# Three longer lags in the order planner of a fused attention and mixture-of-experts kernel

## The chip, the cores and the metric

The kernel runs on one core of a Trainium2 chip. The metric is the device time of one execution in microseconds (us); lower is better. The engines are TensorE (PE), ScalarE (ACT), VectorE (DVE), GpSimd (POOL) and SyncE (SP), and each works off a queue of its own in order.

## The reference

Three layers follow each other on 1152 tokens (2 batches of 576) of width 512:

```
scores = q @ k.T / 8                      # 2 batches, 8 heads, 576 x 576
keep the 32 largest of each row, softmax over them, x = attn @ v
x = prelu(x @ w_in, alpha) @ w_out        # 512 -> 2048 -> 512
logits = x @ w_gate + log1p(exp(x @ w_noise)) * noise
the top 2 of 8 experts for each token, weights = softmax over the two
out[token] = sum over its two experts e: weight * (relu(x @ w1[e]) @ w2[e])   # 512 -> 1024 -> 512
```

## The kernel before

**An order planned in Python.** The kernel writes no schedule by hand. Each piece of work is a Python generator that yields steps: `(engine, cost, lag, ...)`, a lock to take, or a mark to wait for. The class `Order` (L135 on) plays these generators through a simulated clock while the kernel is being built. An engine that is free in the simulation takes the waiting step with the lowest rank. The step's instructions are emitted at that moment, so the order of the simulation becomes the order of each engine's queue on the chip. In `dispatch` the generator's next step becomes known only after the step's cost, a small hop, and the lag:

```
wait = HOP if nxt[0] != eng else STEP if eng in (DVE, ACT, POOL) else 0.0
self.at(end + wait + (req[2] if len(req) > 2 else 0.0), 0, lambda: self.handle(p, nxt))
```

A lag is therefore a guess at how long a transfer takes after its issue. It does not become an instruction. The waits that the chip performs come from the data dependencies, whatever the plan assumed. Costs and lags are constants near the top of the file, in us.

**The expert stage.** Attention and the first layer fill roughly the first 580 us. Then the eight experts follow each other, each with up to 336 tokens in slots. TensorE works in the same pattern for each expert `e` in eight blocks: the hidden part (`expert_block`, L1506, into the banks `h_ps` and `s_ps` in turn), then the output part (L1541, `y` and `x_ps`; L1548 for expert 7). Values are split in two float32r halves, so ACT makes `hh` from a hidden bank (L1517), DVE the rest `hl` (L1522), and both feed the output part. ACT and DVE also split the experts' weights (`w2i`, `w2o`, L1297 and L1300). The steps for `hh` and `hl` carry a rank lowered by 50 and go first where the planner has a choice.

Three round trips through DRAM run beside this:

- *Input rows* (`gather_x`). GpSimd gathers an expert's rows from `x2` into `xg` (L1322). For experts 2 to 7 SP then moves them, quarter by quarter, into the buffers `xh0`, `xl0` (lock `x0`, L1339). After the lag XW, DVE transposes them (L1349), and ACT and DVE split them into the expert's input `xeh` and `xel` (L1364, L1366).
- *Partner rows* (`gather_partner`). Each token has two experts. When expert `e - 1` is in `ysc`, GpSimd gathers for expert `e` those rows that the tokens' other expert produced earlier (L1579). After a lag of DG + GX, ACT scales them with the partner's weight (L1587).
- *Own rows* (`expert_out`). For experts 1 to 6 the output stands transposed. DVE turns it in blocks (L1608), SP writes it to `ysc` (L1615) and reads it back in row order into `wo0`, `wo1` (L1625). After a lag, DVE multiplies with the own weight and adds the partner part (L1636), and GpSimd scatters the sum to the output (L1667).

The gathers of L1322 use the lag GX as well; it stays as it is.

Of the kernel before, what the change touches and what calls it, by code (L numbers as in the profile page):

```python
# [62 lines left out]
MB, MP = 0.0, 0.0  # L63
FILL = 0.8
FS = 3.0
XC, XR, NX, GX, XW = 0.65, 30.0, 2, 5.0, 2.5
XN, LC = 60.0, 35.0
YT = (1, 7)
GB3, NRW = 2, 5
DG, DX, DS = 1.0, 2.0, 0.5  # L70
YC, YL = 0.65, 4.0
NK, FB1 = 4, 12.0
BEGIN = (("DMA", 1.7), ("ACT", 1.9), ("DVE", 1.5), ("POOL", 1.0))


# [33 lines left out]
PE, ACT, DVE, POOL, DMA = "PE", "ACT", "DVE", "POOL", "DMA"  # L109
# [5 lines left out]
def act(n, bias=0):  # L115
    return 0.1 + n * 0.00083 + 0.09 * bias
# [6 lines left out]
def dve(n):  # L123
    return 0.07 + n / 960
# [6 lines left out]
def rows(j):  # L131
    return min(CP, CAP - j * CP)


class Order:  # L135
# [99 lines left out]
    def take(self, *names, room=1):  # L235
        def got():
            for w in names:
                if self.held.get(w, 0) < room:
                    self.held[w] = self.held.get(w, 0) + 1
                    return w  # L240
        return "until", got

    def give(self, what):
        self.held[what] -= 1
        self.given[what] = self.now
        self.at(self.now, 1, self.scan)

    def mark(self, *what):
        self.made.add(what)
        self.at(self.now, 1, self.scan)  # L250

    def need(self, *what):
        return "until", lambda: what in self.made
# [9 lines left out]
def block_kernel(ctx: ExitStack, tc: tile.TileContext, q, k, v, w_in, w_out, alpha,  # L263
# [19 lines left out]
    order = Order()  # L283
    for eng, t in BEGIN:
        order.free[eng] = t
# [1277 lines left out]
    def pieces(*tags):  # L1563

        ts = [split(a2.tile([128, 2, 512], R32, name=t)) for t in tags]
        return [ts[0][:, 0], ts[0][:, 1], ts[1][:, 0]]

    def gather_partner(e):

        yield need("b1")  # L1570
        yield need("ysc", e - 1)
        tags = ("wi0", "wi1") if e % 2 else ("wi2", "wi3")
        for t in tags:
            yield take(t)
        PG[e] = pieces(*tags)
        mv = room["mv"]
        for j in range(CJ):
            yield POOL, 1.04
            nc.gpsimd.indirect_dma_start(  # L1579
                out=PG[e][j][0:rows(j)], out_offset=None, in_=ysc[0:e * WIDTH + 1],  # L1580
                in_offset=bass.IndirectOffsetOnAxis(ap=mv[0:rows(j), e, j, 2:3], axis=0),
                bounds_check=e * WIDTH, oob_is_err=False)
        yield DMA, DG, GX
        for j in range(CJ):
            yield ACT, act(512)
            r = rows(j)
            nc.scalar.activation(PG[e][j][0:r], PG[e][j][0:r], AF.Copy, scale=mv[0:r, e, j, 4:5].bitcast(F32))  # L1587
        yield FIN
        mark("pg", e)

    def to_ysc(e, own):

        yv = ysc[1 + e * WIDTH:1 + (e + 1) * WIDTH]
        nc.sync.dma_start(yv[0:2 * CP].rearrange("(j p) d -> p j d", p=CP), own[:, 0:2])
        nc.sync.dma_start(yv[2 * CP:CAP], own[0:CAP - 2 * CP, 2])

    def expert_out(e):
        turned = YT[0] <= e < YT[1]
        if e < E - 1 or turned:
            yield need("y2d", e, 7)  # L1600
        if turned or not e:
            yield take("yo", room=2)
            yo = room["b1"].tile([128, CJ, DM], F32, name="yo", bufs=2)
        if turned:
            t = yo.rearrange("p j d -> p (j d)")[:, 0:4 * WIDTH].rearrange("p (n b i) -> p n b i", b=4, i=32)
            for b in range(4):
                yield DVE, dve(WIDTH)
                V.transpose(t[:, :, b, :], YP[e][b][:, 0:WIDTH].rearrange("p (n s) -> p n s", s=32))  # L1608
            yield FIN
            give("y")  # L1610
            give("x_ps")
            yv = ysc[1 + e * WIDTH:1 + (e + 1) * WIDTH].rearrange("(n s) d -> s n d", s=32)
            for q in range(4):
                yield "issue", YC
                nc.sync.dma_start(yv[:, :, 128 * q:128 * q + 128], t[32 * q:32 * q + 32].rearrange("p n b i -> p n (b i)"))  # L1615
            yield DMA, DX, YL
            yield FIN
            mark("ysc", e)
            for w in ("wo0", "wo1"):
                yield take(w)  # L1620
            own = pieces("wo0", "wo1")
            yv = ysc[1 + e * WIDTH:1 + (e + 1) * WIDTH]
            yield DMA, 1.5, 2.0
            for j in range(CJ):
                nc.sync.dma_start(own[j][0:rows(j)], yv[j * CP:j * CP + rows(j)])  # L1625
            give("yo")
        if e:
            yield need("pg", e)
        for j in range(CJ):
            r = rows(j)  # L1630
            if e == E - 1 and not turned:
                yield need("y7", j)
            if e:
                yield DVE, dve(512)
                own_j = own[j][0:r] if turned else YP[e][j][0:r]
                V.scalar_tensor_tensor(PG[e][j][0:r], own_j, room["mv"][0:r, e, j, 1:2].bitcast(F32), PG[e][j][0:r],  # L1636
                                       op0=OP.mult, op1=OP.add)
                order.add(ranks["out", e], scatter_out(e, j, PG[e][j]))
            else:
                if j < NE:  # L1640
                    yield need("st", e)
                yield ACT, act(512)
                nc.scalar.activation(yo[0:r, j, :], ST[e] if j < NE else YP[e][j][0:r], AF.Copy)
        yield FIN
        if not turned:
            give("y")
        else:
            give("wo0")
            give("wo1")
        if not turned and e + 1 < E:  # L1650
            yield DMA, 2.1, YL
            to_ysc(e, yo)
            yield "lag0", 0.1
            yield FIN
            mark("ysc", e)
        if not e:
            give("yo")
        if e:
            for j in range(CJ):
                yield need("out", e, j)  # L1660
            for t in ("wi0", "wi1") if e % 2 else ("wi2", "wi3"):
                give(t)

    def scatter_out(e, j, res):
        mv = room["mv"]
        yield POOL, 1.04
        st = nc.gpsimd.indirect_dma_start(  # L1667
            out=out, out_offset=bass.IndirectOffsetOnAxis(ap=mv[0:rows(j), e, j, 3:4], axis=0),
            in_=res[0:rows(j)], in_offset=None, bounds_check=N - 1, oob_is_err=False)
        for o in out_sc:  # L1670
            tc.declare_no_dep(st.ins, o.ins, reason="every row is written once")
        out_sc.append(st)
        yield DMA, DS, 2.0
        yield FIN
        mark("out", e, j)
# [145 lines left out]
    for e in range(E):  # L1821
        te = t + e * TE
        if e < NX:
            ranks["xe", e] = te - 12.0
            order.add(te - 12.0, x_parts(e))
        if e >= NH:
            order.add(te - (XR if e >= NX else XN), gather_x(e))
        for ch in range(4):
            for half in range(2):
                order.add(te + (2 * ch - 4 + half) * FB, weights2(e, ch, half))  # L1830
        for fb in range(8):
            order.add(te + fb * FB, expert_block(e, fb))
        if e:
            order.add(te + 4 * FB, gather_partner(e))
        ranks["out", e] = te + TE
        order.add(te + TE, expert_out(e))
# [221 lines left out]
```

## Time and profile before

| what | value |
|---|---|
| median of 3 runs | 821.95 us (821.02 to 824.26) |
| profiled execution | 821.84 us, of which the span is 820.1 us |
| TensorE busy | 756.5 us, 92% |
| VectorE busy | 607.2 us, 74% |
| ScalarE busy | 506.8 us, 62% |
| GpSimd busy | 356.9 us, 44% |
| mean granted clock of TensorE | 0.965 |

The span reaches from the first to the last instruction of the profiled execution. The engines overlap, so their busy times don't add up to it. A row of a timeline is one instruction, or a few alike; what stands in brackets is the time for which its engine stood idle before it and what it waited for. The table of waits gives for each pair the total in us, how often, and the longest.

### The profile page before, as it was taken

What the parts mean: (1) busy time and instruction counts of PE and PEld (TensorE: products, weight loads), DVE (VectorE), ACT (ScalarE), POOL (GpSimd) and SP (SyncE); (2) the same over time, 40 slices, a digit from 0 to 9 for tenths busy, and PEclk for the clock granted to TensorE, in tenths of its full rate; (3) what the DMA queues carried; (4) which work ended last, traced back from release to release, by engine and by line L of the source; (5) the groups of instructions that cost most, each with busy time, mean ns of one, the idle gap of its engine ahead of it and who ended that gap; (6) DMA issues with size and microseconds to landing.
All of it is one profiled execution on the core that took longest, in us unless ns stands there. A gap on an engine that the chain in (4) does not pass through costs nothing. (4 is left out here: it accounts for less than half of the span.)

```text
span 820.1 us, 15508 instructions
## 1 busy us (share of the span) xinstructions
PE 756.5 (92%) x5238; PEld 690.0 (84%) x5238; DVE 607.2 (74%) x1713; ACT 506.8 (62%) x1081; POOL 356.9 (44%) x402
## 2 busy tenths in 40 slices
PE   8999878779999999999999999989797999999994
PEld 6888867668898998899988988778797999999983
DVE  6999989998988888988899353366547667767541
ACT  6878897887598778576657443454435455545430
POOL 3654665665575554464445334304231243312331
PEclk9999898778999999999999999999998999999998
DMA  9444689851445403573366388969896888986640
GB/s 272 137 154 121 193 290 306 282 181 66 129 164 183 144 26 104 168 240 132 107 191 219 128 242 315 326 179 234 211 244 174 237 258 233 277 234 187 190 125 32
DMA packets 99851, 156.62 MB, mean 191 GB/s; under 512 B 15902, under 2 KB 65582, under 8 KB 99764
## 3 DMA queue, kind: packets, MB, share of 16 engines
q1 hardware_dynamic: 94260, 145.04, 57.6%
q0 software_dynamic: 5504, 10.51, 4.4%
q8 instruction: 43, 0.70, 0.4%
q14 instruction: 44, 0.36, 0.1%
HBM read 126.76 MB, written 29.34 MB: 190 GB/s over the span
## 5 line engine op out<-in xcount | busy, mean ns | idle before, releaser
L671 POOL TENSOR_TENSOR low<-s_sb,low 128x576 f32<-128x576 f32 x72 | 102.4, 1423 | 82.1 <-ACT low L669 80.5
L947 PE MATMUL h_ps<-xh,wi 128*128 128x256 f32 (+1 forms) x576 | 124.0, 295 | 3.0 <-DVE gf L965 2.2
L947 PEld LDWEIGHTS h_ps<-xh,wi 128*128 128x128 f32 x576 | 97.9, 196 | 8.5 <-DVE gf L965 4.3
L632 DVE MAX8 tk<-rest 128x8 f32<-128x296 f32 x216 | 97.8, 459 | 1.1
L991 PE MATMUL y<-wo,gh 128*128 128x512 f32 x288 | 95.9, 414 | 0.2
L978 POOL TENSOR_TENSOR gl<-gf,gh 128x256 fp32r<-128x256 f32 (+1 forms) x80 | 56.5, 709 | 67.3 <-ACT gh L975 65.0
L716 PE MATMUL x_ps<-vb,pT 128*128 128x64 f32 (+1 forms) x640 | 81.0, 273 | 4.1 <-ACT pT L695 3.7
L716 PEld LDWEIGHTS x_ps<-vb,pT 128*128 128x128 f32 (+1 forms) x640 | 76.0, 190 | 10.3 <-ACT pT L695 7.0
L947 PE MATMUL h_ps<-xl,wi 128*128 128x256 f32 (+1 forms) x288 | 83.4, 290 | 0.0
L1297 ACT ACTIVATE w2o<-raw 128x512 fp32r<-128x512 f32 (+1 forms) x60 | 40.4, 710 | 62.2 <-PE x_ps L1541 46.4
L1300 DVE TENSOR_TENSOR w2o<-raw,w2o 128x512 fp32r<-128x512 f32 (+1 forms) x60 | 45.6, 792 | 39.2 <-ACT w2o L1297 38.9
L1541 PE MATMUL y<-hh,w2o 128*128 128x336 f32 (+1 forms) x288 | 68.1, 321 | 6.8 <-ACT hh L1517 6.8
L635 DVE MATCH_REPLACE8 rest<-tk,rest 128x296 f32<-128x296 f32 x144 | 64.9, 451 | 0.0
L1506 PE MATMUL h_ps<-xeh,w2i 128*128 128x336 f32 (+1 forms) x256 | 64.7, 314 | 0.0
L675 ACT ACTIVATE low<-low,bias 128x576 f32<-128x576 f32 x72 | 55.7, 773 | 12.1 <-POOL low L671 12.1
L581 PE MATMUL s_ps<-kp,qt 128*128 128x288 f32 (+2 forms) x336 | 61.2, 311 | 1.7 <-DVE rest L615 1.7
L1506 PE MATMUL s_ps<-xeh,w2i 128*128 128x336 f32 (+1 forms) x256 | 62.1, 310 | 0.0
L597 ACT ACTIVATE s_sb<-s_ps 128x576 f32<-128x576 f32 x72 | 46.8, 650 | 23.5 <-PE s_ps L581 22.9
L1579 POOL DMA_INDIRECT wi<-ysc,meta x21 | 25.1, 1195 | 82.7 <-DMA ysc<-yo 62.9
L669 ACT ACTIVATE low<-s_sb,bias 128x576 f32<-128x576 f32 x72 | 55.6, 774 | 8.8 <-POOL bias L640 8.7
L991 PE MATMUL y<-wo,gl 128*128 128x512 f32 x144 | 58.0, 403 | 2.0 <-POOL gl L978 1.9
L947 PEld LDWEIGHTS h_ps<-xl,wi 128*128 128x128 f32 x288 | 56.6, 197 | 0.7 <-issue 0.3
(315 smaller groups left out, 2077.0 us busy)
## 6 DMA issues: line engine op xcount, KB each, us to landing
raw<-in_moe_w_dram SPq DMA_DIRECT2D x60, 512.0 KB, 4.5
wi<-wsc SPq DMA_DIRECT2D x48, 512.0 KB, 4.3
wo<-wsc SPq DMA_DIRECT2D x48, 512.0 KB, 4.2
raw<-in_moe_w_in_dram SPq DMA_DIRECT2D x16, 512.0 KB, 4.4
raw<-in_moe_w_out_dram SPq DMA_DIRECT2D x16, 512.0 KB, 4.2
wsc<-wi SPq DMA_DIRECT2D x16, 512.0 KB, 4.2
wsc<-wo SPq DMA_DIRECT2D x16, 512.0 KB, 3.9
raw<-in_moe_w_dram SPq DMA_DIRECT2D x48, 128.0 KB, 5.4
```

The lines of the kernel that those rows point to most:

```text
L581: nc.tensor.matmul(s_ps[:, j, o:o + c1 - c0], l, r[:, c0:c1], start=(i == 0), stop=(i == len(steps) - 1 and (c < 4 or c1 != S)))
L632: V.max(tk[:, 8 * i:8 * i + 8], src)
L635: V.match_replace(rest, tk[:, 8 * i:8 * i + 8], src, -3.0e38)
L669: nc.scalar.activation(low, SC[ht], AF.Relu, bias=bi[:, 1:2], scale=-BIG)
L671: nc.gpsimd.tensor_sub(low, SC[ht], low)
L675: nc.scalar.activation(low, low, AF.Exp, bias=bi[:, 0:1], scale=SCALE, accum_out=SM[part][:, col:col + 1])
L716: nc.tensor.matmul(o, pT[:, i, cs], vb[b, hh // 2][:, s, i * 64:(i + 1) * 64], start=(first and hh == h and i == 0), stop=False)
L947: nc.tensor.matmul(h_ps, l[:, d, :], r[:, d, 0:gn], start=(n == 0), stop=(n == 11))
L978: nc.gpsimd.tensor_sub(gl, gf, split(gh))
L991: nc.tensor.matmul(Y1[g][t], l[:, t * 128:(t + 1) * 128], r, start=(i == 0 and n == 0), stop=(i == 15 and n == 2))
L1506: nc.tensor.matmul(h_ps, l[:, d, s * 128:(s + 1) * 128], r[:, d, :], start=(n == 0), stop=(n == 11))
L1541: nc.tensor.matmul(YP[e][b][:, 0:c], l[:, s, bs], r[:, 0:c], start=(fb == 0 and n == 0), stop=(fb == 7 and n == 2))
```

## The change

Three lags of the plan become longer. XW, the lag after the moves of gathered rows, goes from 2.5 to 4.0. The lag after the partner gathers was GX, 5.0, and is now a constant of its own, PL, of 10.0. The lag after the own rows are read back was 2.0, and is now OL, 8.0. No instruction is added, taken away or altered; the order in the engines' queues may differ from the first affected step on.

```diff
-XC, XR, NX, GX, XW = 0.65, 30.0, 2, 5.0, 2.5
+XC, XR, NX, GX, XW = 0.65, 30.0, 2, 5.0, 4.0
...
+OL, PL = 8.0, 10.0
...
                 in_offset=bass.IndirectOffsetOnAxis(ap=mv[0:rows(j), e, j, 2:3], axis=0),
                 bounds_check=e * WIDTH, oob_is_err=False)
-        yield DMA, DG, GX
+        yield DMA, DG, PL
         for j in range(CJ):
             yield ACT, act(512)
...
             yv = ysc[1 + e * WIDTH:1 + (e + 1) * WIDTH]
-            yield DMA, 1.5, 2.0
+            yield DMA, 1.5, OL
             for j in range(CJ):
                 nc.sync.dma_start(own[j][0:rows(j)], yv[j * CP:j * CP + rows(j)])
```

## Rows read from the trace of the kernel before

**Rows 1.** The page: its first line.

```profile
span 820.1 us, 15508 instructions
```

**Rows 2.** Stretches: busy us by engine, then granted clock, DMA share, GB/s.

```profile
650.00:680.00 30.00, 27.44 (x176) 26.61 (x175) 22.18 (x39) 14.04 (x27) 15.40 (x13) 1.00 0.90 278
680.00:710.00 30.00, 30.00 (x198) 30.00 (x197) 22.26 (x38) 15.48 (x29) 11.49 (x10) 1.00 0.89 251
```

**Rows 3.** The table of waits from 585 us to the end.

```profile
ACT wi L1587 <- DMA wi<-ysc,meta: 10.0, 3, 6.9
...
PE y L1541 <- ACT hh L1517: 6.8, 2, 6.1
...
DVE wi L1636 <- DMA wo<-ysc: 5.8, 3, 3.3
...
PE y L1541 <- DVE hl L1522: 2.9, 3, 1.5
...
DVE xl L1349 <- DMA raw<-in_moe_w_dram: 0.9, 1, 0.9
```

**Rows 4.** TensorE's timeline: start us, us, instruction [idle before it <- releaser].

```profile
619.67 0.65 PE L1541 MATMUL y<-hh,w2o 128*128 128x336 f32 x1 [6.05 <-ACT hh L1517]
...
624.95 0.40 PE L1506 MATMUL h_ps<-xeh,w2i 128*128 128x336 f32 x1
...
653.19 0.42 PE L1541 MATMUL y<-hl,w2o 128*128 128x336 f32 x1 [1.46 <-DVE hl L1522]
...
668.71 0.57 PE L1541 MATMUL y<-hh,w2o 128*128 128x336 f32 x2 [0.78 <-ACT hh L1517]
...
739.71 0.42 PE L1541 MATMUL y<-hl,w2o 128*128 128x336 f32 x1 [1.13 <-DVE hl L1522]
```

**Rows 5.** ACT's timeline around the first stall.

```profile
615.27 0.72 ACT L1587 ACTIVATE wi<-wi,meta 128x512 f32<-128x512 f32 x1 [6.93 <-DMA wi<-ysc,meta]
616.60 0.72 ACT L1587 ACTIVATE wi<-wi,meta 128x512 f32<-128x512 f32 x1 [0.61 <-DMA wi<-ysc,meta]
...
619.52 0.43 ACT L1517 ACTIVATE hh<-s_ps 128x336 fp32r<-128x336 f32 x1
...
621.10 0.30 ACT L1364 ACTIVATE xeh<-xl 128x128 fp32r<-128x128 f32 x1
```

**Rows 6.** DVE's timeline around the second and the last stall.

```profile
650.77 0.75 DVE L1636 SCALAR_TENSOR_TENSOR wi<-wo,meta,wi 80x512 f32<-80x512 f32 x1 [0.22 <-DMA wo<-ysc]
...
738.49 0.75 DVE L1636 SCALAR_TENSOR_TENSOR wi<-wo,meta,wi 128x512 f32<-128x512 f32 x1 [3.33 <-DMA wo<-ysc]
```

**Rows 7.** ACT's timeline around the third stall.

```profile
666.05 0.72 ACT L1587 ACTIVATE wi<-wi,meta 80x512 f32<-80x512 f32 x1 [2.50 <-DMA wi<-ysc,meta]
```

**Rows 8.** The tile wo: its loads' times from issue to landing.

```profile
DMA to landing us min/median/max: 2.9/4.9/6.8
```

**Rows 9.** GpSimd's timeline around the first stall.

```profile
603.65 1.40 POOL L1322 DMA_INDIRECT xg<-x,meta  x1 [16.93 <-DMA raw<-in_moe_w_dram]
...
607.95 1.02 POOL L1579 DMA_INDIRECT wi<-ysc,meta  x1 [0.31 <-issue]
...
610.82 0.97 POOL L1579 DMA_INDIRECT wi<-ysc,meta  x1 [0.30 <-issue]
```

**Rows 10.** Line 1579: its gathers' times from issue to landing.

```profile
DMA to landing us min/median/max: 3.0/5.1/7.3
```

**Rows 11.** ACT's and TensorE's timelines at the input of expert 7.

```profile
753.46 0.30 ACT L1364 ACTIVATE xeh<-xl 128x128 fp32r<-128x128 f32 x1
...
777.78 0.32 PE L1506 MATMUL h_ps<-xeh,w2i 128*128 128x336 f32 x1
```

**Rows 12.** ACT's and DVE's timelines at the end.

```profile
797.74 1.94 ACT L1587 ACTIVATE wi<-wi,meta 128x512 f32<-128x512 f32 x3
...
805.26 0.45 ACT L1517 ACTIVATE hh<-s_ps 128x336 fp32r<-128x336 f32 x1 [1.39 <-PE s_ps L1506]
...
807.35 0.75 DVE L1636 SCALAR_TENSOR_TENSOR wi<-y,meta,wi 128x512 f32<-128x512 f32 x1 [1.09 <-PE y L1548]
```

## The prediction, made before the changed kernel was run

> **What bounds the kernel now.** I read the page first: one core, a span of 820.1 us [rows 1], TensorE (PE) busy nearly everywhere. The change touches three kinds of transfer, all of them in the expert stage (experts 1 to 7), so nothing that is planned before about 585 us can move. In that stage the windows show TensorE full at the full granted clock wherever nothing stalls it: 30.00 us busy of 30 at 680 to 710, but 27.44 of 30 at 650 to 680 [rows 2]. So there the time is TensorE's work plus its stalls, and a removed stall is worth its length.
>
> The table of waits lists those stalls: `y` matmuls (L1541) waited 6.8 us for ACT's `hh` (L1517) and 2.9 us for DVE's `hl` (L1522), and nothing else stopped TensorE between 585 us and the end. The same table shows ACT at the partner rows (L1587) waiting 10.0 us in three waits for a DMA, DVE at the returned rows (L1636) 5.8 us in three, DVE at the moved rows (L1349) 0.9 us in one [rows 3]. Each engine takes its instructions in the order of its queue, so an `hh` or `hl` that stands behind such a waiting instruction waits too.
>
> I then followed each TensorE stall back on the timelines [rows 4]:
> - 613.62 to 619.67, 6.05 us. ACT reached the first L1587 of expert 1 at 615.27 - 6.93 = 608.34 and stood there until the partner rows landed; the `hh` that TensorE wanted came only at 619.52, behind all three L1587, although its own input was finished at 613.62 [rows 5].
> - 653.19, 1.46 us. DVE's three L1636 of expert 1 had waited for `wo<-ysc`; the last ran at 650.77, and `hl` came behind it [rows 6].
> - 668.71 and just after, 0.78 + 0.32 us. ACT's third L1587 of expert 2 waited 2.50 us to 666.05 [rows 7].
> - 739.71, 1.13 us. DVE's L1636 of expert 4 waited 3.33 us to 738.49, and the `hl` stood behind it [rows 6].
>
> Together 6.05 + 1.46 + 0.78 + 0.32 + 1.13 = 9.74 us. (6.8 + 2.9 = 9.7 in the table, and the 0.32 is 2.9 less the other two.) All of it hangs on exactly the transfers whose lags change.
>
> **The change part by part.** No instruction is added or taken away; the lags are numbers in the plan, and a longer one only makes the planner give the engine other work first. Every duration stays; what changes is who stands behind whom.
>
> *OL, 2 to 8 us: rows that return from DRAM.* The plan used to hold L1636 back for 1.5 + 2.0 = 3.5 us from the start of the issues; the trace has 2.9 to 6.8 us from issue to landing, median 4.9 [rows 8]. With 9.5 us the slowest is covered with 2.7 us to spare. The longest wait seen, 3.33 us, is under the 6 us added, so both stalls of DVE go: 1.46 + 1.13 = 2.59 us. What moves with L1636 is the scatter on GpSimd (L1667) behind it, six microseconds later; the next instruction there is a later gather, and an output row is wanted by nobody on the chip. Nothing is late next unless the three L1636 (0.75 us each [rows 6]) now fall in front of another `hl`: between 0 and 2.2 us an expert. At the position before, a wait is what made them harmful; I take 0.
>
> *PL, 5 to 10 us: partner rows.* For expert 2 the wait of 2.50 us [rows 7] is under the 5 us added: 0.78 + 0.32 = 1.10 us go. For expert 1 the wait was 6.93 us, and 5 us don't cover it. The reason is GpSimd: its gather of `xg` stood 16.93 us for a buffer and began at 603.65, so the partner gathers started at 607.95, the last at 610.82 [rows 9], and with the landing times of that gather, 3.0 to 7.3 us [rows 10], the last rows are there by 610.82 + 7.3 = 618.1. In the new order ACT comes to the first L1587 at about 608.34 + 5 = 613.3. The `hh` of the second hidden block is ready at 613.62 and has the better rank, so it goes in front or one instruction behind, and TensorE runs its two output blocks (24 matmuls, 3.6 us at the 198 in 30.00 us of [rows 2]) to 613.62 + 3.6 = 617.2. Then expert 2 starts and wants its input tiles (`xeh`, `xel`). Those were finished just after ACT's last L1364 at 621.10 [rows 5], while TensorE came for them at 624.95 [rows 4]: a slack that the stall itself had paid for. If the last two L1364 stay behind the three L1587, the tiles are done at 618.1, plus 0.7 for that L1587, 0.3 for the smaller L1364 [rows 5], and, estimated from these, 0.4 for the larger and 0.3 for DVE's part: 619.8, and TensorE stands for 619.8 - 617.2 = 2.6 us. If they go in front: 0. I take 1.5, nearer the upper end, because the third part pushes them back too. So this part gives 6.05 - 1.5 = 4.55 us for expert 1.
>
> One rule speaks against PL and OL. The Trainium skill's "DMA: Bandwidth & Descriptors", section "Anatomy of one DMA — SWDGE (gpsimd) path", puts a transfer at about 2.0 us plus its bytes over 436 GB/s; for 128 rows of 2 KB that is, as an estimate, 2.6 us, so that both old lags would do. By it the first partner rows would be there at 607.95 + 1.02 + 2.6 = 611.6, the new position of L1587 would wait for nothing, the 1.5 us would fall away and the sum would be 812.1. The trace disagrees in this busy stretch (5.1 and 4.9 us at the median), and I go by it.
>
> *XW, 2.5 to 4 us: moved rows.* It held DVE up once, 0.9 us, and TensorE never; worth 0. Its cost is that the `x0` buffers are given back 1.5 us later for each of six experts, 9 us at most for expert 7. That expert's last L1364 was at 753.46 and TensorE wanted it at 777.78 [rows 11]: 24 us of cover. Without cover it would cost the excess. Only expert 2 is tight, and that is in the 1.5 us above.
>
> *The end.* L1587 of expert 7 moves from 797.74 to about 803, around the last `hh` at 805.26; its result is wanted at 807.35 [rows 12]. Three take 1.94 us, so at worst the last `hh` is delayed by 0.7 us, behind matmuls that still run: 0, bound 0.7.
>
> **Sum.** Against the profiled execution's 821.84 us (span 820.1 plus 1.74 around it, 0.1 under the median of 821.95): 821.84 - 2.59 - 1.10 - 4.55 = 813.6 us, 1.0% less.
>
> **Rivals.**
> - *All goes*: expert 2's tiles are in time. 821.84 - 9.74 = 812.1. For it: five of the six waits at L1587 and L1636 are shorter than what is added. Against: the slack of expert 2 came from the stall.
> - *Handed on*: expert 2 waits the full 2.6 us, and two of the moved groups stall an `hl` again, at the two prices seen, 1.46 and 1.13. 812.1 + 2.6 + 1.46 + 1.13 = 817.3. For it: a new order is a new set of neighbours. Against: at 680 to 710 the same mix ran without any stall.
> - *Hidden anyway*: the weights' stream sets the pace, and TensorE, no longer stalled at L1587, waits for weights instead: 821.8. For it: the DMA share is 0.90 at 650 to 680 [rows 2]. Against: in that stage no row has TensorE waiting for a weight, and the stream kept up at 680 to 710 with TensorE full.
> - *Slower*: the L1636 group, now planned blind into the middle of a block, stands whole in front of an `hl` that TensorE wants, in each of experts 1 to 6. Price 3 x 0.74 = 2.2 us each, 13.3 in all: 813.6 + 13.3 = 826.9. It decides from the point where the loss passes the 8.2 us gained, that is four groups of six. For it: 650.77 [rows 6]. Against: that group had waited, and the plan ranks `hl` far ahead of L1636.
>
> **How the numbers follow.** A measurement of this kernel tells about 0.5%, 4.1 us, from no change: faster is under 817.8, slower over 826.1. Chances: forecast 0.45, all goes 0.12, handed on 0.18 (it lies at that border: half faster, half same), hidden 0.18, slower 0.07. That gives faster 0.66, same 0.27, slower 0.07. The range: from 811.5, just under "all goes", to 820.5, which takes in "handed on" and the lower part of "hidden"; that is 8 in 10. The forecast's own range is 812 to 815.
>
> **What would show it.** Right: no wait at L1636 for `wo<-ysc`; L1587's waits for expert 1 down from 6.93 + 0.61 to about 2 us with `hh` in front; TensorE's stalls in the stage down from 9.74 to about 1.5 us, and that at the start of expert 2, for `xeh` or `xel`; everything before about 585 us as before; TensorE's last matmul some 8 us earlier. Wrong: stalls of TensorE for `hl` right behind L1636, waits of ACT for weights, or a new long wait of GpSimd in front of a partner gather, which would bring the wait at L1587 back at its new place.

## The result, and the profile after

| | median | lowest to highest | runs |
|---|---|---|---|
| kernel before | 822.24 us | 821.02 to 826.88 | 5 |
| changed kernel | 811.89 us | 810.85 to 814.54 | 5 |

The ratio is 0.9878, with a 95% interval of 0.9842 to 0.9914: 10.0 us less, between 7 and 13. A ratio is estimated from the single runs that lie within 1.5% of the fastest of their kernel, so it is not the quotient of the two medians. The profiled execution took 811.02 us. In the changed kernel every line from L73 on has a number higher by one: L1587 is L1588 there, L1636 is L1637. The page of the changed kernel [rows 1]:

```profile
span 809.3 us, 15510 instructions
## 1 busy us (share of the span) xinstructions
PE 752.3 (93%) x5238; PEld 685.8 (85%) x5238; DVE 606.2 (75%) x1713; ACT 506.4 (63%) x1081; POOL 358.1 (44%) x402
```

Each engine has as many busy instructions as before (the two more in the first line are not among them). The table of waits over the expert stage, the lines that answer to [rows 3]:

```profile
PE s_ps L1507 <- DVE hl L1523: 3.8, 1, 3.8
...
ACT wi L1588 <- DMA wi<-ysc,meta: 1.2, 2, 0.7
...
PE y L1549 <- ACT hh L1518: 0.5, 1, 0.5
...
PE h_ps L1507 <- DVE hl L1523: 0.4, 1, 0.4
```

All the `y` stalls of L1541 are gone, and so is the wait of DVE for `wo<-ysc`. ACT waits 1.2 us for partner rows where it waited 10.0. But 3.8 us of TensorE's waiting is new. ACT's timeline around expert 1's partner rows [rows 5] shows how the first part worked:

```profile
608.81 0.45 ACT L1518 ACTIVATE hh<-s_ps 128x336 fp32r<-128x336 f32 x1 [1.22 <-PE s_ps L1507]
609.15 0.41 ACT L1365 ACTIVATE xeh<-xh 128x256 fp32r<-128x256 f32 x1
...
610.41 0.30 ACT L1365 ACTIVATE xeh<-xl 128x128 fp32r<-128x128 f32 x1
611.40 0.72 ACT L1588 ACTIVATE wi<-wi,meta 128x512 f32<-128x512 f32 x1 [0.69 <-DMA wi<-ysc,meta]
612.63 1.34 ACT L1588 ACTIVATE wi<-wi,meta 128x512 f32<-128x512 f32 x2 [0.51 <-DMA wi<-ysc,meta]
...
614.92 0.43 ACT L1518 ACTIVATE hh<-h_ps 128x336 fp32r<-128x336 f32 x1
...
678.93 1.15 ACT L1298 ACTIVATE w2o<-raw 128x512 fp32r<-128x512 f32 x2 [3.54 <-PE h_ps L1507]
679.98 0.40 ACT L1365 ACTIVATE xeh<-xh 128x256 fp32r<-128x256 f32 x1
680.29 0.43 ACT L1518 ACTIVATE hh<-s_ps 128x336 fp32r<-128x336 f32 x1
```

Both `hh` and the last two splits of expert 2's input stand ahead of the partner rows now, so what is left of the wait no longer delays them. It still delays the next `hh`, at 614.92, whose block had ended at 614.04 on TensorE's timeline, and the 0.4 us that TensorE waits for `h_ps` at 616.30 comes behind that. The last three lines belong to the new stall, on TensorE's timeline at the start of expert 3:

```profile
673.58 0.31 PE L1542 MATMUL x_ps<-hl,w2o 128*128 128x336 f32 x1
...
677.65 0.32 PE L1507 MATMUL h_ps<-xeh,w2i 128*128 128x336 f32 x1
681.75 0.42 PE L1507 MATMUL s_ps<-xeh,w2i 128*128 128x336 f32 x1 [3.78 <-DVE hl L1523]
```

ACT stood 3.54 us ahead of a weight conversion (`w2o`, L1298), and the `hh` that TensorE's next block needs came behind it at 680.29. This wait was not for the load of these weights. ACT's queue takes the load's semaphore in an instruction of its own, and was through it at 674.7; the load had been issued at 663.80. It is the first of the two in this group of L1298, from 674 to 680 us:

```profile
L1298 ACTq EVENT_SEMAPHORE  x2: 17/17/17, 674.7 to 679.8; - x2
```

What the conversion itself waits for is a semaphore of TensorE, as in 17 other waits of the stage, which the end of an output part (`x_ps`) ended. The last output part had ended at 673.89 by TensorE's timeline, above. But the trace has five updates of that semaphore close together, from 678.80 to 679.16, and ACT went on at 678.93. So the signal came some 5 us behind the recorded end of the matmul; in the kernel before, every such update follows its matmul within 0.3 us. Why it came late is not shown. This trace also lacks records: it has 650 updates of TensorE's semaphore, the one of before has 674. The stretches of the changed kernel [rows 2] show what the transfers did then (the columns end with granted clock, DMA share, GB/s):

```profile
650.00:680.00 30.00, 27.97 (x180) 27.29 (x178) 15.96 (x28) 10.91 (x21) 9.98 (x10) 1.00 0.87 235
680.00:710.00 30.00, 28.25 (x174) 28.26 (x175) 20.72 (x37) 15.91 (x32) 4.53 (x5) 0.94 0.87 234
665.00:670.00 5.00, 5.00 (x34) 5.00 (x34) 4.39 (x7) 1.32 (x3) 3.48 (x4) 1.00 1.05 343
670.00:675.00 5.00, 5.00 (x35) 5.00 (x34) 2.19 (x5) 2.07 (x5) 4.09 (x4) 1.00 1.07 323
675.00:680.00 5.00, 2.97 (x17) 2.29 (x15) 2.52 (x4) 1.47 (x5) 2.29 (x3) 1.00 0.80 181
680.00:685.00 5.00, 3.25 (x13) 3.26 (x14) 4.59 (x10) 4.14 (x9) 0.00 (x0) 0.72 0.64 163
685.00:690.00 5.00, 5.00 (x33) 5.00 (x32) 2.90 (x5) 2.02 (x4) 0.00 (x0) 0.94 1.01 262
```

The DMA engines were full from 665 to 675, just ahead of the stall; that the one led to the other is not shown. After it TensorE ran at a mean granted clock of 0.72, partly at the lower of its two levels (1.2 of 2.4 GHz): 13 matmuls took 3.25 us, where at 35 in 5.00 they take 1.86, so about 1.4 us went there, and by the 33 matmuls of the next window 0.3 us more.

**Where the time went.** The kernel before has such a low clock too, behind its 6.05 us stall. Its stretches there, not shown so far:

```profile
620.00:625.00 5.00, 5.00 (x26) 4.84 (x25) 3.21 (x7) 1.40 (x3) 0.53 (x1) 0.71 0.67 208
625.00:630.00 5.00, 5.00 (x35) 4.88 (x34) 4.46 (x14) 2.68 (x5) 2.48 (x3) 1.00 0.58 141
```

26 matmuls ran where the next window has 35. From the first of them at 619.67 to the start of expert 2 at 624.95 [rows 4] the two output blocks took 5.28 us, where the prediction has 3.6 at the full clock: 1.7 us more. So stalls and low clock cost 9.74 + 1.7 = 11.4 us before, and 3.8 + 0.5 + 0.4 + 1.7 = 6.4 us after: 5.0 us less. The stage itself, from the first output matmul of expert 1 to the end of the span, is shorter by about that, 5.3 us: 820.1 - 591.2 = 228.9 us before, 809.3 - 585.7 = 223.6 after. The starts are from the groups of that line (duration in ns, first and last start, shapes), of the kernel before:

```profile
L1541 PE MATMUL y<-hh,w2o x288: 308/317/650, 591.2 to 777.0; 128*128 128x336 f32 x126, 128*128 128x352 f32 x18
```

and of the changed kernel, which has no matmul of 650 ns among them:

```profile
L1542 PE MATMUL y<-hh,w2o x288: 309/316/408, 585.7 to 767.4; 128*128 128x336 f32 x126, 128*128 128x352 f32 x18
```

The other 5.5 us of the 10.8 between these two spans came ahead of the stage, where every queue has the same order in both kernels (the first difference on any engine is at 599.8 us). The changed order can't have made them; over the runs below, this arrival scatters by more than ten microseconds.

### The profile page after: what moved, and what is told of

Same layout as the page of the kernel before. It is cut to its first block, busy times and chain, and to the rows that moved or that the text cites. A ratio compares the mean times of both kernels' runs of the same rounds, so it can differ in the third digit from the quotient of the medians.

```text
span 809.3 us, 15510 instructions
## 1 busy us (share of the span) xinstructions
PE 752.3 (93%) x5238; PEld 685.8 (85%) x5238; DVE 606.2 (75%) x1713; ACT 506.4 (63%) x1081; POOL 358.1 (44%) x402
## 5 line engine op out<-in xcount | busy, mean ns | idle before, releaser
L1298 ACT ACTIVATE w2o<-raw 128x512 fp32r<-128x512 f32 (+1 forms) x60 | 40.4, 711 | 57.2 <-PE x_ps L1542 31.6
L1507 PE MATMUL s_ps<-xeh,w2i 128*128 128x336 f32 (+1 forms) x256 | 64.9, 315 | 3.8 <-DVE hl L1523 3.8
L1323 POOL DMA_INDIRECT xg<-x,meta x21 | 25.7, 1225 | 72.2 <-DMA xl<-xg 28.9
```

Of the source, the lines that this page charges most:

```text
L1507: nc.tensor.matmul(h_ps, l[:, d, s * 128:(s + 1) * 128], r[:, d, :], start=(n == 0), stop=(n == 11))
```

## The experiments

Each batch was timed against the kernel before, run beside it. Its medians were 821.54 us (816.82 to 828.38), 822.76 (817.14 to 827.99) and 821.87 (813.58 to 829.66), of 29 runs each. The experiments have the line numbers of before. "O", "P" and "X" below are the three parts: OL 8, PL 10, XW 4.

| kernel | median us (lowest to highest, runs) | ratio, 95% interval | first `y` of expert 1 | stage |
|---|---|---|---|---|
| O alone | 821.34 (815.72 to 827.86, 12) | 0.9993 (0.9959 to 1.0027) | 589.9 | 231.9 |
| P alone | 814.80 (809.40 to 819.02, 12) | 0.9920 (0.9888 to 0.9953) | 583.0 | 225.6 |
| X alone | 818.74 (814.82 to 822.21, 12) | 0.9960 (0.9931 to 0.9990) | 595.2 | 222.1 |
| before again | 819.90 (one) | | 588.4 | 229.7 |
| L1587 without its wait | 814.49 (809.26 to 823.20, 12) | 0.9910 (0.9875 to 0.9946) | 588.0 | 221.4 |
| O and P | 818.11 (813.32 to 823.10, 12) | 0.9947 (0.9915 to 0.9978) | 590.2 | 223.8 |
| P and X | 817.76 (814.89 to 821.83, 12) | 0.9950 (0.9923 to 0.9977) | 593.4 | 221.6 |
| changed kernel again | 813.47 (807.59 to 816.48, 6) | 0.9882 (0.9833 to 0.9931) | 589.3 | 224.6 |
| no wait at L1587, and O | 810.77 (806.73 to 814.00, 6) | 0.9887 (0.9838 to 0.9936) | 590.9 | 220.0 |
| P for expert 1 alone | 816.89 (812.97 to 822.57, 12) | 0.9955 (0.9917 to 0.9992) | 599.3 | 218.5 |
| longer still: PL 14, OL 12 | 815.44 (809.54 to 818.79, 12) | 0.9937 (0.9906 to 0.9969) | 596.8 | 220.2 |
| changed, six raw buffers | 814.03 (805.74 to 819.10, 12) | 0.9905 (0.9865 to 0.9944) | 594.8 | 216.8 |

The last two columns are of the one profiled execution. A late arrival mostly goes with a shorter stage, so a whole span, or a stage, of one profile does not rank these kernels; the ratios do, as far as their intervals reach.

### The three parts, each alone

```diff
-            yield DMA, 1.5, 2.0
+            yield DMA, 1.5, 8.0      # O alone
...
-        yield DMA, DG, GX
+        yield DMA, DG, 10.0          # P alone
...
-XC, XR, NX, GX, XW = 0.65, 30.0, 2, 5.0, 2.5
+XC, XR, NX, GX, XW = 0.65, 30.0, 2, 5.0, 4.0   # X alone
```

**O alone**, expected:

> Only OL goes from 2 to 8; XW and PL stay at 2.5 and 5. Theory of the prediction (a lag that is too short puts a waiting instruction in front of work that TensorE wants): the stalls behind the own rows go, about 2.6 us (1.46 + 1.13), so a ratio near 0.997, and the 6 us stall of expert 1 behind the partner rows stays. Rival (the gain comes from elsewhere, since the changed kernel's profiled execution was already 5.5 us ahead at the first output matmul of expert 1, where both orders are still the same): no relation to which lag is changed, 1.000 with the waits at the own rows gone all the same.

No wait at L1636 for `wo<-ysc` is left, as forecast, and the time did not move measurably. What was freed went to the next wait in line. The timelines of this kernel, ACT's at the start of expert 3:

```profile
663.45 0.72 ACT L1587 ACTIVATE wi<-wi,meta 80x512 f32<-80x512 f32 x1 [2.90 <-DMA wi<-ysc,meta]
664.08 0.43 ACT L1517 ACTIVATE hh<-s_ps 128x336 fp32r<-128x336 f32 x1
```

and TensorE's:

```profile
665.10 0.42 PE L1506 MATMUL s_ps<-xeh,w2i 128*128 128x336 f32 x1 [2.44 <-DVE hl L1522]
```

The order had shifted so that expert 2's last L1587 stood in front of an `hh` needed at once: 2.44 us, and a granted clock of 0.67 from 665 to 670 us. The long stall of expert 1 stood too (7.2 us). TensorE's stalls add up to 10.2 us in this kernel, against 9.74 before, so by the trace the 2.59 us of the prediction's sum are not had from O alone. The times by themselves don't exclude them: 2.59 us less would be a ratio of 0.9968, inside the interval.

**P alone**, expected:

> Only PL is new, 10 in place of 5; XW and OL stay at 2.5 and 2. Theory: the stalls of expert 1 and expert 2 behind the partner rows go, 6.05 + 1.10 us and some 1.7 us in which the clock stood lower after the long stall, so about 8.9 us, ratio near 0.989; the waits at the own rows stay, 2 to 3 us of stalls. Rival (gain from elsewhere): 1.000.

L1587 waited once, 2.08 us, and both `hh` stood ahead of it. The start of expert 2 was late for its tiles, as the prediction's term for expert 1 has it. TensorE's timeline:

```profile
610.21 0.42 PE L1506 MATMUL h_ps<-xeh,w2i 128*128 128x336 f32 x1 [1.10 <-ACT xeh L1364]
...
611.47 0.65 PE L1506 MATMUL h_ps<-xel,w2i 128*128 128x336 f32 x1 [0.85 <-DVE xel L1366]
```

and ACT's, with one split left behind the wait:

```profile
608.28 0.72 ACT L1587 ACTIVATE wi<-wi,meta 128x512 f32<-128x512 f32 x1 [2.08 <-DMA wi<-ysc,meta]
...
609.86 0.29 ACT L1364 ACTIVATE xeh<-xl 128x128 fp32r<-128x128 f32 x1
```

1.95 us, inside the prediction's 0 to 2.6. DVE's waits at L1636 remain, and 3.5 us of stalls for `hl`.

**X alone**, expected:

> Only XW goes from 2.5 to 4; OL and PL stay at 2 and 5. Theory: TensorE never waited for the moved rows, so nothing is gained, 0.995 to 1.005, and the long wait at the partner rows of expert 1 is there again. Rival (every new order that differs from this one does better, since this one had bad luck at expert 1): a gain of 4 us or more here too.

The prediction gave X nothing; it gives 0.4% (0.9931 to 0.9990). It reorders more than its own step: in this kernel a `w2o` conversion and one more of expert 2's splits come ahead of the first L1587, and an `hh` between the L1587, which waited only 1.8 us in all; the last two splits (619.82 and 621.07) stay behind them. Its profile also arrived late at the stage (595.2), which shortens that wait; how much is order and how much arrival isn't separated.

### The wait at L1587 itself

First the kernel before once more, the lags unchanged:

> The kernel before, unchanged, for a second profile of it. If the 5.5 us that the changed kernel was ahead at the start of expert 1 are chance between executions, this execution reaches the first output matmul of expert 1 somewhere else than at 591.2, by microseconds, with the same order of instructions, while the stalls of 6.05, 1.46, 1.10 and 1.13 us behind the partner rows and the own rows come again at the same instructions. If they belong to the kernel, it reaches it at 591 again.

Then the same kernel, in which L1587 scales an idle tile, so that every queue keeps its order and only the wait is gone; it leaves out the scaling of the partner part:

```diff
-            nc.scalar.activation(PG[e][j][0:r], PG[e][j][0:r], AF.Copy, scale=...)
+            nc.scalar.activation(ST[0][0:r], ST[0][0:r], AF.Copy, scale=...)
```

> All lags as before, and every queue in the order of before, instruction for instruction; only L1587 scales an idle tile in place of the gathered partner rows, so that ACT has nothing to wait for there (the partner part of the output is left unscaled). Theory (the cost is ACT standing at L1587 with hh behind it): the stalls of expert 1 and 2 behind it go, with the low clock after the long one, 9 us at most, and up to 2.6 us come back at the start of expert 2: a ratio of 0.989 to 0.993. Rival (what helps is another order, not the missing wait): 1.000.

ACT's timeline in the kernel before, second profile:

```profile
605.05 0.41 ACT L1364 ACTIVATE xeh<-xh 128x256 fp32r<-128x256 f32 x1
614.60 1.47 ACT L1587 ACTIVATE wi<-wi,meta 128x512 f32<-128x512 f32 x2 [9.14 <-DMA wi<-ysc,meta]
...
617.33 0.71 ACT L1587 ACTIVATE wi<-wi,meta 80x512 f32<-80x512 f32 x1
617.94 0.43 ACT L1517 ACTIVATE hh<-h_ps 128x336 fp32r<-128x336 f32 x1
618.27 0.43 ACT L1517 ACTIVATE hh<-s_ps 128x336 fp32r<-128x336 f32 x1
```

and in the kernel without the wait:

```profile
604.74 0.41 ACT L1364 ACTIVATE xeh<-xh 128x256 fp32r<-128x256 f32 x1
605.05 1.47 ACT L1587 ACTIVATE st<-st,meta 128x512 f32<-128x512 f32 x2
...
608.12 0.71 ACT L1587 ACTIVATE st<-st,meta 80x512 f32<-80x512 f32 x1
608.74 0.43 ACT L1517 ACTIVATE hh<-h_ps 128x336 fp32r<-128x336 f32 x1
610.45 0.45 ACT L1517 ACTIVATE hh<-s_ps 128x336 fp32r<-128x336 f32 x1 [1.28 <-PE s_ps L1506]
```

The same instructions in the same order, on every engine: in the first, TensorE stood 7.21 us for that `hh` (to 618.42), in the second not at all, and the time falls by 0.9%. Both reach the stage at 588 us, and the stage is 8.3 us shorter. This is the cause of the long stall, shown apart from any change of order. The stall comes back in both profiles of before (6.05 and 7.21 us), as do the ones behind L1636 of expert 1 (1.46 and 1.15) and L1587 of expert 2 (0.78 + 0.32 and 0.97 + 0.31); the 1.13 us of expert 4 did not come again.

### Two parts together, and the whole again

O and P, X as before:

> OL 8 and PL 10, XW at the old 2.5. By the prediction, which gave XW nothing, this is the whole gain: 0.987 to 0.989. Rival (XW earns part of it, as its own run of 0.996 suggests): about 0.992, like PL alone.

The start of expert 2 is late by 1.5 + 0.8 us, for `xeh` and `xel`; no wait for `wo<-ysc` is left. The ratio, 0.9947, came out above both expectations. P and X, O as before:

> PL 10 and XW 4, OL at the old 2. By the prediction 2.6 us of the gain are missing here: 0.991. Rival (OL earns nothing, as its own run of 0.999 suggests): as good as all three, 0.987 to 0.989, and waits at L1636 that cost little.

Nothing is late at expert 2, and L1587 never waits; L1636 waits 6.0 us in three, with 1.9 us of stall behind it. Here all splits of expert 2 stand ahead of L1587, as in the changed kernel; P alone leaves the last one behind it. That nothing is late is not the order's doing alone, since L1587 did not wait. The ratio, 0.9950, is above the 0.991 expected, though the stage is 8.1 us shorter than in the second profile of before; why the time does not show that is open. The changed kernel once more:

> The changed kernel again, for a second profile and more times (its constants stand on one line, so the line numbers are those of the kernel before). Its first profile had a new stall of 3.8 us at the start of expert 3, after a late weight conversion on ACT, while the DMA engines were full. If that belongs to the new order it comes again at the same place; if it is chance, it does not. The ratio should be 0.988 again.

The ratio agrees, 0.9882, and the new stall at expert 3's start is there again, on TensorE's timeline:

```profile
685.41 0.65 PE L1506 MATMUL s_ps<-xeh,w2i 128*128 128x336 f32 x1 [2.65 <-DVE hl L1522]
```

again behind a `w2o` conversion ahead of which ACT stood 3.09 us, again after a DMA share of up to 1.12, and with a granted clock of 0.50 behind it. Here too ACT's queue was through the semaphore of the load (678.8), and five updates of TensorE's semaphore came together, from 682.47 to 682.83, while ACT went on at 682.60. This trace lacks records as well, with 656 updates. So do those of L1587 without its wait, of O and P and of P and X (650 to 653), without such a stall; the traces of all other kernels have 674.

### Other ways to take the wait away

The kernel without the wait, and OL 8:

> OL 8, the other lags old, and L1587 on an idle tile as in the run without that wait (the partner part of the output is left unscaled). Theory (OL alone earned nothing because the wait at the partner rows of expert 2 took over what OL freed): with that wait gone, OL is worth its 2.3 to 2.6 us, no stall of TensorE behind L1636 is left in the trace, and the ratio is 0.988, 0.3% under the run without OL (0.991). Rival (OL is worth nothing in itself): 0.991 again, with stalls for hl at other places.

Its stalls behind L1587 and L1636 are gone and its ratio is that of the changed kernel, but it can't be told from the kernel without the wait alone (0.9875 to 0.9946). Its one large stall shows what X may guard against. DVE's timeline:

```profile
624.47 0.84 DVE L1349 STREAM_TRANSPOSE xl<-xl 128x640 f32<-128x640 f32 x1 [2.58 <-DMA xl<-xg]
...
626.78 0.49 DVE L1522 SCALAR_TENSOR_TENSOR hl<-h_ps,hh 128x336 fp32r<-128x336 f32 x1
```

DVE stood at the moved rows, with XW still 2.5, and TensorE waited 2.64 us, to 627.33, for the `hl` behind them. Then P for expert 1 alone:

```diff
-        yield DMA, DG, GX
+        yield DMA, DG, 10.0 if e == 1 else GX
```

> PL 10 for expert 1 alone; the partner rows of experts 2 to 7 keep 5, OL and XW are old. Theory (nearly all of PL's gain is the one long stall of expert 1): 0.992 to 0.993, as PL for all. Rival (the gain is spread over the experts): 0.996 or more.

0.9955 (0.9917 to 0.9992) against 0.9920 for P alone: the intervals overlap, so how the gain of P splits over the experts is not settled. L1587 waited 0.4 us, and expert 2 started in time, although its last split stands behind the first L1587 as in P alone; this profile reached the stage latest of all.

### Past the change

Longer lags still (PL 14, OL 12, XW 4), and the changed kernel with a sixth buffer for raw weights:

```diff
-GB3, NRW = 2, 5
+GB3, NRW = 2, 6
```

> All three and longer: PL 14, OL 12, XW 4. Theory: at 10 and 8 the waits at L1587 and L1636 are already under 2 us together and cost TensorE nothing, so there is nothing left to earn: 0.986 to 0.991, like the changed kernel, and the stall at the start of expert 3 stays, or moves with the new order. Rival (more lag is more gain): under 0.985.

> The changed kernel with a sixth buffer for raw weights (NRW 6 in place of 5), so that loads can be issued earlier. Theory (the changed kernel's stall of 2.6 to 3.8 us at the start of expert 3 comes from a weight load that lands late while the DMA engines are full): ACT's wait of 3 us before its w2o conversion there goes, and with it the stall and the low clock behind it: 4 us, ratio to before 0.983. Rival (late for another reason, or the new order brings stalls of its own): 0.988 or more.

In both, TensorE's only stall in the stage is 0.54 us at the end. The sixth buffer at the place of the new stall:

```profile
675.00:680.00 5.00, 5.00 (x35) 5.00 (x34) 3.66 (x7) 2.46 (x5) 4.05 (x4) 1.00 1.05 337
680.00:685.00 5.00, 5.00 (x34) 5.00 (x34) 4.88 (x12) 3.33 (x8) 4.09 (x4) 1.00 1.09 274
```

TensorE is full at the full clock although the DMA engines are as busy as in the changed kernel. So a high DMA share by itself does not bring the stall. It does not speak for late weights either, the theory of the expectation: the traces of the changed kernel show that the load had landed. The sixth buffer also alters the order earlier in the program, and the traces of these two kernels lack no records; which of these differences took the stall away is not shown.

Neither kernel is measurably faster than the changed one (0.9937 with the longer lags, 0.9905 with the sixth buffer, against 0.9878 and 0.9882). Of the 4 us and more of stalls that the longer lags remove, 3.3 us come back at the end. The scatters of expert 6 (L1667) wait behind the later L1636 and stand in front of those of expert 7. GpSimd's timeline has the last one at

```profile
808.33 0.92 POOL L1667 DMA_INDIRECT out_dram<-wi,meta  x1 [0.30 <-issue]
```

5.0 us after TensorE's last output matmul ended (803.31), and in the changed kernel, 1.7 us after it (798.84), at

```profile
800.56 0.93 POOL L1668 DMA_INDIRECT out_dram<-wi,meta  x1 [0.31 <-issue]
```

The sixth buffer has no such end, and its stage is the shortest of all profiles; what it gains there is not found again in the time, and that stays open.

## Why the prediction was right, and where it was not

- **The cause.** Right, and shown: an engine that stands at rows in flight holds up the `hh` or `hl` behind it. Removing the wait alone, in the same order, gives 0.9910.
- **PL for expert 1, 4.55 us.** The direction was right, two sizes were off. The 6.05 us stall was priced at its length; with the low clock after it, it cost 6.05 + 1.7. And the 1.5 us kept for a late start of expert 2 did not fall due: 1.95 and 2.4 us of it stand in P alone and in O and P, nothing in those with X, where the wait at L1587 was also shorter (0 to 1.8 us in all, against 2.1 and 2.2). The prediction's reason for taking the upper end, that XW pushes the splits back, was wrong in sign: together with P, the longer lag moved the plan so that the last split comes ahead of L1587.
- **OL, 2.59 us, and PL for expert 2, 1.10 us.** Both waits went. But the parts don't add up: O alone gives nothing that can be measured, since expert 2's L1587 (and a low clock) took the place of what it freed. With P beside it that wait is gone too. That an output row is wanted by nobody on the chip holds at OL 8 (10.4 us from the last output matmul to the end, 10.7 before) and not at OL 12 (13.7).
- **XW, 0.** Wrong: alone it gives 0.4%, and 2.64 us of stall at L1349 show what the old lag allowed once the other waits were gone. In the trace of before, TensorE had no stall for it; whether longer ones hid it is not shown.
- **The end, 0.** 0.54 us of stall appeared there, within the bound of 0.7, but not by way of L1588, which stood behind the `hh` in question. What changed is the order of TensorE's last blocks. Before, the last two hidden blocks stand together, so that the `hh` of the last is made while another output block runs. Now an output block stands between them, and the output block of the last hidden block, which ended at 795.16, follows at once and waits for its `hh`:

```profile
795.70 0.73 PE L1549 MATMUL y<-w2o,hh 128*128 128x512 f32 x2 [0.54 <-ACT hh L1518]
```

- **What was not foreseen** in the sum is the stall at expert 3's start: 3.78 and 2.65 us, and a low clock behind it. It came at a weight conversion, but neither by a late load, which was on the prediction's list as "waits of ACT for weights", nor by a moved group, as in "handed on", whose size it has: ACT waited there for a signal of TensorE that came late, for a reason that stays open.
- **The rivals.** "Slower" fell: L1637 stood directly in front of an `hl` that began at 639.38 and of one at 765.24, and TensorE waited for neither. "Hidden" fell: both intervals lie below 1. "All goes" (812.1) is nearest in time to the 811.89, but not by its mechanism: the stalls of before did all go, and about half as much came back.

By the stage's own account (5.3 us, and 229.7 - 224.6 = 5.1 us in the second pair) the gain is smaller than the 8.2 us predicted. By the ratios it is 7 to 13 us, and 5.7 to 13.7 in the repetition. The scatter ahead of the stage lies between the two accounts; what is left of the difference is not settled. Nor is the order among P, O and P, P and X, and the last two kernels, whose intervals overlap. One possibility, not shown, is that the new stall, which both profiles have, is not in every run: with its low clock it is 5.5 us in the first. That the median came within 2 us of the forecast is in part luck: of the terms of the sum one was too small, one did not fall due, and two stalls came that it lacks.

## What to carry to other kernels

Where an order planned ahead becomes an in-order queue, a lag must cover the slow end of the landing times in the trace, because a wait costs what stands behind it: the next wanted instruction, and the clock after it where that falls. More than that is not better: the longest lags here moved work to the end of the kernel. Judge such lags together, since the gain of one alone may go to the next wait in line. And compare stalls and stage lengths of profiles, not their spans, when what lies ahead of the stage scatters more than the effect.

## What the runs showed of the hardware

**Landing times under load.** Gathers of 128 or 80 rows landed in 3.0 to 7.3 us and reads of `ysc` in 2.9 to 6.8 [rows 8, 10]; the profile has a landing for 15 of the 21 gathers and 6 of the 18 reads. In the changed kernel ACT got the first partner rows at 611.40, above. GpSimd's timeline has their gather at 603.79, again behind a long wait [rows 9]:

```profile
599.47 1.42 POOL L1323 DMA_INDIRECT xg<-x,meta  x1 [17.91 <-DMA xl<-xg]
...
603.79 1.22 POOL L1580 DMA_INDIRECT wi<-ysc,meta  x1 [0.30 <-issue]
```

That is 7.6 us from the start of the gather and 6.4 from its end, so even the new lag was used up. The Trainium skill's "DMA: Bandwidth & Descriptors", section "Anatomy of one DMA — SWDGE (gpsimd) path", puts a transfer at about 2.0 us plus its bytes over 436 GB/s, as an estimate 2.6 us for the 256 KB of this gather; this trace disagrees, at a DMA share of 0.93 from 600 to 625 us. The section is on GpSimd's path, so for the reads of `ysc`, which SyncE issues, it gives no price.

**The clock behind a stall.** Stalls of 6.05, 3.78 and 2.65 us were followed by granted clocks of 0.71, 0.72 and 0.50 in the window of five microseconds behind them. The length of a stall alone doesn't tell this. One of 2.64 us in the kernel without the wait and OL 8, which ended at 627.33, left the clock where it was, and so did one of 2.56 us in X alone (to 646.23, clock 1.00 from 645 to 655), while after 2.09 us in L1587 without its wait (to 643.55) the clock was 0.66 from 643 to 648:

```profile
625.00:630.00 5.00, 2.67 (x17) 2.67 (x18) 4.97 (x10) 1.40 (x3) 3.28 (x3) 1.00 0.90 254
```

The row is that of the kernel without the wait and OL 8.

**A signal behind its matmul.** In the two profiles of the changed kernel, the update of TensorE's semaphore that let ACT go on came about 5 us behind the recorded end of the last output part (673.89 and 678.90, 677.14 and 682.57). The ends of matmuls are modelled and these traces lack records, so how much of this is the chip is not shown.

**The same order doesn't arrive at the same time.** Kernels whose queues are alike up to 599 us reached expert 1's first `y` between 583.0 and 599.3 us, and the kernel before took 813.58 to 829.66 us over the 29 runs of the last batch. Why is not shown.
